# The end of the kernel-spectrum stage of an S4D and mixer block: sums ahead of inverse products, and other PSUM banks for the last pieces

## The chip, the cores and the metric

The kernel runs on one core of one Trainium2 chip. The metric is the device time of one execution in microseconds (us). A core has TensorE (PE; its weight loads are listed as PEld), VectorE (DVE), ScalarE (ACT), GpSimd (POOL) and SyncE (SP, which here only issues DMAs). SBUF is the on-chip memory, and PSUM is the small memory that TensorE writes its results to. A profile is one execution as the hardware profiler recorded it.

## The reference

For a sequence of 2048 tokens with 448 channels, a state-space convolution (S4D) and a token-mixing MLP follow each other, each behind a layer norm with a modulation from a condition vector:

```
dt = exp(log_dt); A = -exp(log_A_real) + 1j * A_imag; C = (C_real + 1j * C_imag) * dt
P = exp((A * dt)[:, :, None] * pos)                    # 448 channels x 256 states x 2048 positions
K = 2 * einsum("dn,dnl->dl", C, P).real                # the convolution kernel of every channel
y = irfft(rfft(h, 4096) * rfft(K, 4096))[:2048] + h * D_skip
x = x + ga * y
h = layernorm(x) * (1 + cb) + sb
x = x + gb * mixer(h)      # layernorm, W1 (2048 x 1792), gelu, W2 (1792 x 2048) along the tokens
```

## The kernel before, in words

**Steps.** The convolution kernel K is made in 56 steps (`NHALF`), two for each of 28 groups of 16 channels. In step s ACT turns two PSUM tiles `xe`, `xg` of phases (pool `pph`, two buffers of two banks each: 4 banks) into sines and cosines (`st_step`, L674), POOL multiplies them into G (L690, L691), DVE into E (L692 to L696), and PE multiplies G and E into `kg` (`st_kgen`, L708; pool `pkg`, 1 bank). After the second step of a group ACT copies `kg` to `ks` (L731), and after each second group POOL adds the skip weights (L737). `st_s1` (L742) then multiplies such a pair of groups into two banks `y` (`y1` in the code) of the pool `pms` (3 banks), whose contents are copied to `yk`, the spectrum of the kernel (L761). `yk` has two chunks of 224 channels; groups 14 to 27, so steps 28 to 55, make the second chunk.

**Pieces.** The product of the spectra and the way back are cut into 32 pieces, 16 for each chunk. Piece n has three parts: the sums `kx` (`pc_s2`, L803, 8 matmuls into one bank of `pms`), the products `z` with the input's spectrum `u` (`pc_mul`, L811, two on DVE), and the inverse products `vv` (`pc_inv`, L821, 8 matmuls) with their copy to `vt` and a DMA to DRAM (`pc_out`, L834). Pieces of the first chunk put `vv` into two banks of `pms` and copy it in two instructions (L842). Pieces of the second put it into a tile of two banks of the pool `pxs` (two buffers) and copy it in one (L839). A piece of the second chunk needs besides a copy of `u` with quarters exchanged (`pc_swap`, L797: two copies on POOL, two on ACT).

**Their order.** PE, ACT, DVE and POOL run in the order of the program. Work that is put off is kept in the lists `dve` and `act`, which `flush` empties at given places of a step; a pair of groups goes to `fresh`, and `mellow` makes it `ready` for `st_s1`. SP's order is chosen by a planner until the second chunk's loop, where from its first round on it is that of the program. The first chunk's pieces run inside steps 33 to 55 by `piece` (L994): an odd step gives the sums of a piece, the next even step its inverse products. The loop over steps (L1081) ran three steps beyond the last (`tail`), in which only pieces and leftovers run. So, in the order of PE:

- step 54: `kg` of step 53, `y` of the pair of groups 24 and 25, `vv` of piece 12 (L1161)
- step 55: `kg` of step 54, `kx` of piece 13
- 56 to 58: `kg` of step 55, then `vv` 13, `kx` 14, `vv` 14, `kx` 15, `y` of the pair 26 and 27, `vv` 15
- second chunk (L1204): `kx` 16, `kx` 17, `vv` 16 and so on

**Loads.** `pc_load(n + 3)` stands ahead of the sums of piece n: `u` (three buffers, 448 KB each, one tile for two pieces in the second chunk) and the table `si` (four buffers, 256 KB). The table of piece n + 4 takes the buffer of piece n, so its load waits for `vv` of n.

After the second chunk come the layer norm and the two products of the mixer, with weights streamed from DRAM (L1270 to L1272, L1433 to L1435).

Of the kernel before, what the change touches and what calls it, by code (L numbers as in the profile page):

```python
# [11 lines left out]
F32 = mybir.dt.float32  # L12
# [4 lines left out]
PSUM = bass.MemoryType.PSUM  # L17
# [5 lines left out]
P = 128  # L23
# [6 lines left out]
NHALF = 2 * NG  # L30
BATCH = 8
DC = 224
NP = 16
# [199 lines left out]
def tile_adaln_s4d_mixer(ctx, tc, i, out):  # L233
# [19 lines left out]
    with ExitStack() as es:  # L253
# [11 lines left out]
        cg, mp, wp = right("cg", 1), right("mp", 8), right("wp", 2)  # L265
        m2p = [right("m2", 3)]
        pms = es.enter_context(tc.tile_pool(name="pms", bufs=3, space=PSUM))
        pph = kgen.enter_context(tc.tile_pool(name="pph", bufs=2, space=PSUM))
        pkg = kgen.enter_context(tc.tile_pool(name="pkg", bufs=1, space=PSUM))
        early = ExitStack()  # L270
        qp = early.enter_context(tc.tile_pool(name="qp", bufs=1))
        mod[0:3] = [qp.tile([P, D], F32, name=f"mod{k}") for k in range(3)]
# [105 lines left out]
        def flush(todo):  # L378
            while todo:
                todo.pop(0)()  # L380
# [323 lines left out]
        def mellow():  # L704
            ready.extend(fresh)
            fresh.clear()
# [32 lines left out]

                act.append(copy)  # L740

        def st_s1(busy):  # L742

            if not ready:
                return False
            p = ready.pop(0)
            c, gl = divmod(p, NG // 4)
            ks = kss.pop(p)
            y1 = [pms.tile([P, 32, 2, 4, 2], F32, tag="ms", name="y1") for _ in range(2)]
            for o in range(2):  # L750
                for m in range(4):
                    for cc in range(2):
                        for q in range(2):
                            r = slice(64 * q, 64 * q + 64)
                            T.matmul(
                                y1[q][64 * cc : 64 * cc + 64, :, o, m], ks[r, o, m], wc[r, cc, r], start=True, stop=True
                            )

            def out(q, copy):
                o = yks[c][:, :, 2 * gl * GD : 2 * (gl + 1) * GD].rearrange("p k (g q m) -> p k g q m", g=2, q=2)  # L760
                copy(o[:, :, :, q], y1[q].rearrange("p k g m b -> p k g (m b)"))  # L761

            for q in range(2):
                (dve if busy else act).append(partial(out, q, V.tensor_copy if busy else S.copy))
            return True


# [22 lines left out]
        def pc_load(n):  # L790
            if n < NP or n % 2 == 0:
                pc_u(n)
            pc_w(n)

        pw = {}

        def pc_swap(n):  # L797

# [20 lines left out]
            pk.pop(n)  # L819

        def pc_inv(n):  # L821
            if n < NP:
                pv[n] = [pms.tile([P, DC], F32, tag="ms", name="vv") for _ in range(2)]
            else:
                pv[n] = pxs.tile([P, 2, 512], F32, tag="vv", name="vv")
            halves_ = pv[n] if n < NP else [pv[n][:, q, 0:DC] for q in range(2)]
            w, z = pl.pop(n), pz.pop(n)
            for t in range(2):
                for b in range(2):
                    for q in range(2):  # L830
                        to, rows = slice(64 * (b ^ q), 64 * (b ^ q) + 64), slice(64 * q, 64 * q + 64)
                        T.matmul(halves_[q][to], w[rows, 1, t, b], z[t][rows, b], start=t == 0, stop=t == 1)  # L832

        def pc_out(n, copy=S.copy):  # L834
            c, p = divmod(n, NP)
            vt = swp.tile([P, 2, DC], F32, tag="vt", name="vt", bufs=4) if c else fp.tile([P, 2, DC], F32, tag="vt", name="vt")
            from_ = pv.pop(n)
            if c:
                copy(vt, from_[:, :, 0:DC])  # L839
# [154 lines left out]
        def piece(go, inside=False):  # L994

            if pieces[1] < pieces[0]:
                n = pieces[1]
                pc_inv(n)
                (dve if inside else act).append(partial(pc_out, n, V.tensor_copy if inside else S.copy))
                pieces[1] += 1  # L1000
            if go:
                n = pieces[0]
                if n + 3 < 2 * NP:
                    pc_load(n + 3)
                pc_s2(n)
                dve.append(partial(pc_mul, n))
                pieces[0] += 1

        def window(s):
# [11 lines left out]
            for e in range(BATCH):  # L1021
# [20 lines left out]
                if s and e < (2 if s <= 32 else 1):  # L1042
                    st_kgen(s - (2 if s <= 32 else 1) + e)
                elif e == 5:
                    if s == 8:
                        yks[0] = y0.tile([P, 32, DC], F32, tag="yk", name="yk0")
                    st_s1(s > 16)
# [29 lines left out]

        WPACE = [[0, 2, 2, 1, 1, 1, 1, 1], [4] * 7 + [8], [4] * 7 + [9], [4] * 8]
        pace = [2] * 32
        tail = NHALF + 3  # L1080
        for s in range(tail):  # L1081
            if s == 32:
                early.close()
                fp = es.enter_context(tc.tile_pool(name="fp", bufs=2))
# [7 lines left out]
                first.close()  # L1092
            if s in late:
                late[s]()
            if s < NHALF and s % BATCH == 0:
                window(s)
                if s == 0:
                    gp_ = right("gp", 3)
# [10 lines left out]
                    more(pace[s])  # L1109

            mellow()
            if s >= NHALF:
                flush(dve)
                mellow()
            else:
                if s < 32 and s % BATCH > 1:
                    st_kgen(s - 2)
                if s % BATCH < 2:
                    warm(10)
                if (s + 1) % BATCH:  # L1120
                    st_phase(s + 1)
                elif s + 1 < NHALF:
                    st_exponents(s + 1)
                if s == 7:
                    warm(10)

                if s > 32 and s % BATCH:
                    st_kgen(s - 1)
                st_step(s, between)
            flush(act)  # L1130
            if s == NHALF:
                st_kgen(s - 1)


            if s in (1, 2):
                x_load(4 + 4 * s, 4, G)
            free = s > 7 and not st_s1(s % BATCH == BATCH - 1)
            if s + 2 < 32 and (s + 2) % BATCH > 1 and s + 2 > 5:
                st_mag2(s + 2)

# [28 lines left out]
        flush(dve)  # L1169
        flush(act)  # L1170
        assert pieces == [NP, NP] and not kss and next(rest, 0) == next(rows, 0) == next(cols, 0) == 0, pieces
# [32 lines left out]
        for k in range(NP + 1):  # L1204
# [262 lines left out]
```

## Time and profile before

| | us |
|---|---|
| three runs | 693.27, 696.14, 698.49 |
| median | 696.14 |
| span of the profiled execution | 693.5 |
| PE busy in it | 628.4 (91%) |
| DVE, ACT, POOL busy | 438.7, 446.6, 269.7 |
| mean granted TensorE clock | 0.968 of full speed |

Of the profiled execution only the span, from its first to its last instruction, is on record, and no time of its own. It lies 0.2 us above the fastest of the three runs and 2.6 us below their median. Busy times are sums over the whole span, in which stages with different limits follow each other; the stage that matters here begins at about 339 us and ends at about 362 us. In a row of a timeline the time in brackets is how long the engine stood idle before the instruction, with the work that released it. A table over stretches of time gives each engine's busy time with the number of its instructions, the granted clock, and the DMA engines' mean busy share.

### The profile page before, as it was taken

How to read it: one execution, taken by the hardware profiler on the slowest of the kernel's cores; microseconds unless marked ns; L12 is line 12 of the kernel's file. 1: busy time of each engine (PE TensorE's matmuls, PEld its weight loads, DVE VectorE, ACT ScalarE, POOL GpSimd, SP SyncE). 2: the span in 40 equal slices, each digit the busy share in tenths (PEclk: the TensorE clock that was granted, in tenths of full speed). 3: DMA queues.
4: the chain of work that ended last, by engine and by line, in shares of the span. 5: the costliest groups of instructions: out<-in, count | busy, mean ns of one | idle time of the engine just before them, and what ended most of it. 6: DMA issues, size and time to landing. Idle time of an engine off the chain costs nothing.

```text
span 693.5 us, 19319 instructions
## 1 busy us (share of the span) xinstructions
PE 628.4 (91%) x7706; PEld 452.3 (65%) x7706; DVE 438.7 (63%) x835; ACT 446.6 (64%) x847; POOL 269.7 (39%) x349
## 2 busy tenths in 40 slices
PE   0878999999888889988898899999999999999997
PEld 0444555444345545555554567778899999999997
DVE  7886789789785574856745578876732364444441
ACT  5888598999689889989856768887322352222220
POOL 7694669588499667767635300000000000000000
PEclk9989999999999899999899999999999999999999
DMA  7595557598786354443479899955574445556540
GB/s 174 176 208 130 196 186 247 200 225 258 219 253 189 94 131 140 131 125 104 116 251 341 280 269 261 262 151 142 177 226 108 146 132 160 160 162 170 163 131 26
DMA packets 100322, 125.16 MB, mean 180 GB/s; under 512 B 13860, under 2 KB 81992, under 8 KB 100232
## 3 DMA queue, kind: packets, MB, share of 16 engines
q1 hardware_dynamic: 99288, 121.30, 61.0%
q0 software_dynamic: 944, 2.62, 1.6%
q8 instruction: 61, 1.00, 0.6%
q14 instruction: 29, 0.24, 0.1%
HBM read 88.53 MB, written 34.87 MB: 178 GB/s over the span
## 4 chain that ended last, share of the span: by engine, by line
PE 62%; ACT 12%; POOL 8%; DMA 6%; DVE 5%; issue 5%; SPq 1%; DVEq 0%; POOLq 0%; ACTq 0%
PE o L1434 7%; PE acc L1270 6%; PE o L1433 6%; PE o L1435 6%; PE acc L1271 6%; PE acc L1272 6%; PE xe L627 5%; PE kg L717 4%; POOL G L691 3%; POOL G L690 2%; PE xg L627 2%; PE vv L832 2%; PE kx L809 2%; PE kg L639 2%; PE y L1307 2%
## 5 line engine op out<-in xcount | busy, mean ns | idle before, releaser
L218 ACT CAST whi<-w 128x896 fp32r<-128x896 f32 x64 | 59.7, 938 | 134.3 <-PE o L1434 82.6
L227 DVE TENSOR_TENSOR wlo<-w,whi 128x896 fp32r<-128x896 f32 x64 | 68.1, 1085 | 40.6 <-ACT whi L218 40.6
L690 POOL TENSOR_TENSOR G<-mag,gs 128x512 f32<-128x512 f32 x56 | 71.8, 1282 | 46.0 <-ACT gs L686 45.9
L1270 PE MATMUL acc<-h3h,whi 128*128 128x448 f32 x224 | 82.9, 370 | 1.7 <-ACT h3h L1337 0.9
L1271 PE MATMUL acc<-h3l,whi 128*128 128x448 f32 x224 | 81.6, 364 | 0.2 <-DVE mean L1291 0.2
L1434 PE MATMUL o<-ul,whi 128*128 128x448 f32 x224 | 81.3, 363 | 0.0
L1433 PE MATMUL o<-uh,whi 128*128 128x448 f32 x224 | 81.2, 362 | 0.0
L1272 PE MATMUL acc<-h3h,wlo 128*128 128x448 f32 x224 | 80.7, 360 | 0.0
L1435 PE MATMUL o<-uh,wlo 128*128 128x448 f32 x224 | 80.6, 360 | 0.0
L717 PEld LDWEIGHTS kg<-E,G 128*32 128x32 f32 x3584 | 58.1, 117 | 31.7 <-issue 22.1
L717 PE MATMUL kg<-E,G 128*32 128x64 f32 x3584 | 68.2, 231 | 4.1 <-issue 4.1
L691 POOL TENSOR_TENSOR G<-mag,gs 128x512 f32<-128x512 f32 x56 | 71.8, 1281 | 0.0
L627 PE MATMUL xg<-tab,lph 64*128 64x512 f32 x112 | 62.9, 561 | 8.0 <-DVE E L696 3.5
L627 PE MATMUL xe<-tab,lph 64*128 64x512 f32 x112 | 63.6, 568 | 1.9 <-ACT gs L687 0.9
L1438 DVE TENSOR_TENSOR y<-o,x 128x448 f32<-128x448 f32 x16 | 10.0, 624 | 78.8 <-PE o L1435 78.8
L692 DVE TENSOR_TENSOR E<-m,xe 128x512 f32<-128x512 f32 x53 | 36.3, 684 | 35.2 <-ACT xe L685 25.1
L671 POOL TENSOR_TENSOR m<-mag,w 128x512 f32<-128x512 f32 x53 | 55.8, 1052 | 4.1
L1270 PEld LDWEIGHTS acc<-h3h,whi 128*128 128x128 f32 x224 | 42.0, 188 | 15.2 <-ACT h L1342 3.5
L817 DVE TENSOR_TENSOR z<-kx,u 128x448 f32<-128x448 f32 x48 | 28.4, 619 | 33.1 <-PE kx L809 30.5
L832 PE MATMUL vv<-z,si 64*64 64x224 f32 x512 | 36.8, 385 | 9.4 <-ACT yk L761 6.2
L627 PE MATMUL xe<-tab,lex 64*128 64x512 f32 x56 | 31.0, 569 | 15.7 <-POOL wm L874 14.8
L1433 PEld LDWEIGHTS o<-uh,whi 128*128 128x128 f32 x224 | 42.1, 188 | 3.4
(242 smaller groups left out, 1455.9 us busy)
## 6 DMA issues: line engine op xcount, KB each, us to landing
w<-in_B_w_dram SPq DMA_DIRECT2D x64, 224.0 KB
w<-in_B_w_dram SPq DMA_DIRECT2D x32, 448.0 KB
yu_d<-yt SPq DMA_DIRECT2D x16, 448.0 KB
yi<-yu_d SPq DMA_DIRECT2D x32, 224.0 KB
us_d<-uo SPq DMA_DIRECT2D x16, 448.0 KB
u<-us_d SPq DMA_DIRECT2D x64, 112.0 KB
v_d<-vt SPq DMA_DIRECT2D x32, 224.0 KB
vt<-v_d SPq DMA_DIRECT2D x14, 448.0 KB
```

Of the source, the lines that this page charges most:

```text
L218: self.nc.scalar.copy(hi, w)
L227: eng.tensor_tensor(lo, w, hi.bitcast(F32), ALU.subtract)
L627: T.matmul(out[k], lhs[r], rhs[r], start=start, stop=stop)
L690: G.tensor_tensor(Gt[:, 1], mg_, v32(sg), ALU.mult)
L691: G.tensor_tensor(Gt[:, 0], mg_, v32(cg_), ALU.mult)
L717: T.matmul(kg[32 * q : 32 * q + 32, m], Gt[:, c, d], E[:, c, d], start=h == 0 and c == 0 and m == 0, stop=h == 1 and c == 1, skip_group_ch ...
L1270: nc.tensor.matmul(acc[f], hi[:, fs], h3h[:, r], start=r == 0, stop=False)
L1271: nc.tensor.matmul(acc[f], hi[:, fs], h3l[:, r], start=False, stop=False)
L1272: nc.tensor.matmul(acc[f], lo[:, fs], h3h[:, r], start=False, stop=r == 15)
L1433: nc.tensor.matmul(o, hi[:, ks], uh[kh][:, k], start=kh == 0 and k == 0, stop=False)
L1434: nc.tensor.matmul(o, hi[:, ks], ul[kh][:, k], start=False, stop=False)
L1435: nc.tensor.matmul(o, lo[:, ks], uh[kh][:, k], start=False, stop=kh == 1 and k == 6)
```

## The change

- The loop ends with step 55 (`range(NHALF)`), and step 54 has no call of `piece`. What steps 55 to 58 did behind `st_step` stands behind the loop as straight code.
- Its order on PE: `kg` of step 54, `kx` 13 (its products now right behind the E products of step 55 on DVE), `kg` of step 55, `vv` 12, `kx` 14, `y` of the pair 26 and 27, `vv` 13, `kx` 15, `vv` 14. `vv` 15 moves into the first round of the second chunk's loop, behind `kx` 16.
- `pkg` moves to the other side of PSUM, and the phases' four banks are given up after step 55 (`phases.close()`). `pxs` takes them at once, and pieces 12 to 15 put their `vv` there and copy it in one instruction.
- The last two copies of `yk` are divided, one on DVE, one on ACT; they were both on ACT.

```diff
-        pph = kgen.enter_context(tc.tile_pool(name="pph", bufs=2, space=PSUM))
-        pkg = kgen.enter_context(tc.tile_pool(name="pkg", bufs=1, space=PSUM))
+        pkg = kgen.enter_context(tc.tile_pool(name="pkg", bufs=1, space=PSUM, side="right"))
+        phases = ExitStack()
+        pph = phases.enter_context(tc.tile_pool(name="pph", bufs=2, space=PSUM))
...
-        def st_s1(busy):
+        def st_s1(*to):
...
             for q in range(2):
-                (dve if busy else act).append(partial(out, q, V.tensor_copy if busy else S.copy))
+                to[-q].append(partial(out, q, S.copy if to[-q] is act else V.tensor_copy))
...
         def pc_inv(n):
-            if n < NP:
-                pv[n] = [pms.tile([P, DC], F32, tag="ms", name="vv") for _ in range(2)]
+            if wide:
+                pv[n] = wide[0].tile([P, 2, 512], F32, tag="vv", name="vv")
+                halves_ = [pv[n][:, q, 0:DC] for q in range(2)]
             else:
-                pv[n] = pxs.tile([P, 2, 512], F32, tag="vv", name="vv")
-            halves_ = pv[n] if n < NP else [pv[n][:, q, 0:DC] for q in range(2)]
+                pv[n] = halves_ = [pms.tile([P, DC], F32, tag="ms", name="vv") for _ in range(2)]
...
-            if c:
+            if not isinstance(from_, list):
                 copy(vt, from_[:, :, 0:DC])
...
-        tail = NHALF + 3
-        for s in range(tail):
+        for s in range(NHALF):
...
                 st_step(s, between)
+            if s == NHALF - 1:
+                break
             flush(act)
-            if s == NHALF:
-                st_kgen(s - 1)
...
-            if s > 32:
-                piece(pieces[0] < NP and (s % 2 == 1 or s >= NHALF))
+            if s > 32 and s != NHALF - 2:
+                piece(s % 2 == 1)
...
+        def forth(n):
+
+            if n + 3 < 2 * NP:
+                pc_load(n + 3)
+            pc_s2(n)
+            pc_mul(n)
+
+        def back(n):
+
+            pc_inv(n)
+            pc_out(n)
+
+        def settle():
+
+            flush(dve)
+            flush(act)
+            flush(dve)
+            mellow()
+            mellow()
+
+        phases.close()
+        pxs = es.enter_context(tc.tile_pool(name="pxs", bufs=2, space=PSUM))
+        wide.append(pxs)
+        n = pieces[0]
+        assert pieces == [NP - 3, NP - 4]
+        forth(n)
         flush(act)
+        st_kgen(NHALF - 1)
+        settle()
+        back(n - 1)
+        forth(n + 1)
+        st_s1(dve, act)
+        for f in dve + act:
+            f()
+        dve.clear()
+        act.clear()
+        back(n)
+        forth(n + 2)
+        back(n + 1)
         kgen.close()
-        pxs = es.enter_context(tc.tile_pool(name="pxs", bufs=2, space=PSUM))
...
-            if k:
-                pc_inv(n - 1)
-                pc_out(n - 1)
+            back(n - 1)
```

More of the change, by code (lines that the diff above doesn't have):

```diff
@@ L793, in pc_load @@
             pc_w(n)
-        pw = {}
+        pw, wide = {}, []
         def pc_swap(n):
@@ L1046, in window @@
                         yks[0] = y0.tile([P, 32, DC], F32, tag="yk", name="yk0")
-                    st_s1(s > 16)
+                    st_s1(dve if s > 16 else act)
                 for k, e0 in ((4, 1), (5, 3), (3, 6)) if s == 16 else ():
@@ L1094, in tile_adaln_s4d_mixer @@
                 late[s]()
-            if s < NHALF and s % BATCH == 0:
+            if s % BATCH == 0:
                 window(s)
@@ L1111, in tile_adaln_s4d_mixer @@
             mellow()
[L1112 to L1115, printed above, removed]
+            if True:
                 if s < 32 and s % BATCH > 1:
@@ L1129, in tile_adaln_s4d_mixer @@
                 st_step(s, between)
+            if s == NHALF - 1:
+                break
             flush(act)
-            if s == NHALF:
-                st_kgen(s - 1)
             if s in (1, 2):
                 x_load(4 + 4 * s, 4, G)
-            free = s > 7 and not st_s1(s % BATCH == BATCH - 1)
+            free = s > 7 and not st_s1(dve if s % BATCH == BATCH - 1 else act)
             if s + 2 < 32 and (s + 2) % BATCH > 1 and s + 2 > 5:
@@ L1168, in tile_adaln_s4d_mixer @@
                 nc.sync.dma_start(b2, i["B_b2"].rearrange("(t p) -> p t", p=P))
-        flush(dve)
-        flush(act)
-        assert pieces == [NP, NP] and not kss and next(rest, 0) == next(rows, 0) == next(cols, 0) == 0, pieces
+        def forth(n):
[18 more added lines that the diff above has]
+        forth(n)
+        flush(act)
+        st_kgen(NHALF - 1)
[10 more added lines that the diff above has]
+        back(n + 1)
+        assert not kss and next(rest, 0) == next(rows, 0) == next(cols, 0) == 0
         kgen.close()
-        pxs = es.enter_context(tc.tile_pool(name="pxs", bufs=2, space=PSUM))
         wst = WeightStream(tc, ctx, i)
```

## Prediction

> **What bounds the kernel now.** I read the page first, then a table of stages, then the timeline from step 54 to the second chunk engine by engine, and last the granted clock in stretches of 3.41 us and the DMA share. In the tables a row gives the stretch, its length, then PE, PEld, DVE, ACT and POOL busy us with their instructions, the granted TensorE clock, the DMA share and GB/s.
>
> ```profile
> span 693.5 us, 19319 instructions
> ...
> 344.60:357.60 13.00, 11.92 (x274) 7.45 (x269) 3.47 (x6) 3.23 (x9) 2.41 (x5) 0.81 0.61 193
> ...
> 405.00:550.00 145.00, 144.20 (x698) 122.51 (x699) 90.10 (x216) 82.72 (x158) 0.00 (x0) 1.00 0.72 193
> ```
>
> From 405 us on PE is the bound (144.2 of 145 us), so a start that comes earlier comes out at the end. The change acts between the last products of step 55 (about 344.6) and the first sums of the second chunk, kx of piece 16 (357.58). In these 13 us PE looks busy, but at a clock of 0.81, while DVE, ACT and POOL are nearly empty. The timeline shows why (start, us, engine, line, work, idle before and its releaser):
>
> ```profile
> 338.49 1.10 PE L717 MATMUL kg<-E,G 128*32 128x64 f32 x64
> ...
> 340.89 0.68 DVE L696 TENSOR_TENSOR E<-m,xg 128x512 f32<-128x512 f32 x1
> 342.92 1.10 ACT L761 COPY yk<-y 128x512 f32<-128x512 f32 x2
> 343.59 1.76 PE L832 MATMUL vv<-z,si 64*64 64x224 f32 x14 [2.50 <-ACT yk L761]
> 343.66 0.68 DVE L696 TENSOR_TENSOR E<-m,xg 128x512 f32<-128x512 f32 x1
> 343.32 1.28 POOL L691 TENSOR_TENSOR G<-mag,gs 128x512 f32<-128x512 f32 x1
> 345.28 1.93 PE L717 MATMUL kg<-E,G 128*32 128x64 f32 x64
> 347.15 1.76 PE L809 MATMUL kx<-yk,si 128*64 128x224 f32 x8
> 348.84 1.46 PE L717 MATMUL kg<-E,G 128*32 128x64 f32 x64
> 350.22 0.99 PE L832 MATMUL vv<-z,si 64*64 64x224 f32 x16
> 350.37 0.37 ACT L731 COPY ks<-kg 128x256 f32<-128x256 f32 x1 [4.38 <-PE kg L717]
> 350.82 0.21 POOL L737 TENSOR_TENSOR ks<-ks,dsk 128x8 f32<-128x8 f32 x1 [6.22 <-ACT ks L731]
> 351.14 0.98 PE L809 MATMUL kx<-yk,si 128*64 128x224 f32 x8
> 352.17 1.16 DVE L817 TENSOR_TENSOR z<-kx,u 128x448 f32<-128x448 f32 x2 [2.05 <-PE kx L809]
> 354.82 1.16 PE L755 MATMUL y<-wc,ks 64*64 64x64 f32 x64
> 356.03 1.07 ACT L761 COPY yk<-y 128x512 f32<-128x512 f32 x2 [1.36 <-PE y L755]
> 356.24 1.41 PE L832 MATMUL vv<-z,si 64*64 64x224 f32 x16 [0.26 <-DVE z L817]
> 357.58 1.73 PE L809 MATMUL kx<-yk,si 128*64 128x224 f32 x16
> 358.36 3.45 ACT L801 COPY sw<-u 32x448 f32<-32x448 f32 x6
> 359.58 0.62 DVE L817 TENSOR_TENSOR z<-kx,sw 128x448 f32<-128x448 f32 x1 [0.34 <-ACT sw L801]
> 360.26 1.15 POOL L801 COPY sw<-u 32x448 f32<-32x448 f32 x2 [3.71 <-DVE z L817]
> 361.82 0.53 ACT L839 COPY vt<-vv 128x448 f32<-128x448 f32 x1
> ```
>
> The reader is to see one wait and its long tail. Inverse products of piece 12 (343.59) wait 2.50 us: the pool pms has three banks, the sums of piece 12 and the two banks of y had them, and the second bank for vv comes free only when ACT, which first has the whole sine chain of step 55 to do, copies yk. Behind that matmul stand, in PE's order, the kg products of step 54, whose E was ready at 341.57 (340.89 + 0.68). Everything then runs at half speed (64 kg matmuls 1.93 us against 1.10) until about 349.6, and the kg products of step 55, ready at 344.60 (POOL's 343.32 + 1.28), end at 350.3 instead of 345.7. After them come the copy of ks, POOL's addition, y, yk. The clock in detail:
>
> ```profile
> 339.42:342.83 3.41, 1.67 (x79) 1.17 (x67) 3.37 (x6) 3.21 (x8) 2.37 (x3) 1.00 0.39 105
> 342.83:346.24 3.41, 2.65 (x50) 1.74 (x54) 1.35 (x3) 1.78 (x5) 1.77 (x2) 0.50 0.14 39
> ...
> 192.64:196.06 3.42, 1.93 (x30) 0.75 (x28) 3.42 (x6) 3.31 (x8) 3.34 (x4) 1.00 1.05 299
> 196.06:199.47 3.41, 3.41 (x120) 2.00 (x114) 3.07 (x6) 1.78 (x4) 3.33 (x5) 1.00 1.09 318
> ```
>
> PE busy 1.67 us of a stretch is followed by half clock, 1.93 us is not. Between these lies the threshold that I use below.
>
> **The change part by part.** I lay out the new order on PE from the times above, with 1.10 us for a kg group and y (1.16, of which the next group hides some), and 0.93 us from one kx or vv group to the next (350.22 to 351.14 gives 0.92).
>
> *Step 54 without a piece.* The inverse products of piece 12 leave the place where they stalled. The kg products of step 54 start at 341.6 and end at 342.7; the sums of piece 13, put ahead of the inverse products, follow to 343.6 (the bank of kx 12 is free once its products are done, which stand on DVE ahead of the E row of 340.89). PE then waits for G of step 55 (344.60). PE is busy about 2.0 us in any 3.41 us here, above 1.93, so I take full clock. Price if not: one stretch of 3.41 us at half speed, 1.7 us.
>
> *After step 55.* kg of step 55 344.65 to 345.7; vv 12 to 346.65; kx 14 to 347.6; y to 348.65; vv 13 to 349.6; kx 15 to 350.5; vv 14 to 351.45; kx 16 from 351.45. Side work: the products of piece 13 on DVE right behind E (344.34 to 345.5, before 348.96); ks on ACT 345.8 to 346.2, POOL's addition to 346.4, 1.2 us before y wants it; products of piece 14 347.65 to 348.8, piece 15 350.55 to 351.7. The copies of yk are split, one on DVE (behind the products of 14), one on ACT, and end at 349.5; kx 16 reads them 2 us later. So none of these is on the path while PE goes from group to group. The same work took until 357.58: 6.1 us earlier.
>
> *The phases' banks as buffers.* vv 12 to 15 get two pairs of banks of their own. They are free when E of step 55 is done (344.34), before vv 12 (345.7). That removes the wait of vv 15 for yk (356.24, 1.41 us) too. One copy of 128x448 (0.53 us, the 361.82 row) takes the place of two; four pieces save a fraction of a us of ACT that is idle anyway. I price the addresses and the moved kg bank at nothing; nothing on the path waits for a bank of that side.
>
> *Piece 15 goes into the second chunk's loop.* Its inverse products follow kx 16 on PE and its copy follows the swaps of 17 on ACT. PE: kx 16 to 352.4, vv 15 to 353.3, kx 17 to 354.2. ACT: vt 14 to 352.05, two swaps of 16 (3.45 us for six, 0.575 each) to 353.2, so the swapped product of 16 starts at 353.25 against 359.58 (6.3 earlier); swaps 17 to 354.35, vt 15 to 354.9, swaps 18 to 356.05, vt 16 at 356.05 against 361.82 (5.8 earlier). POOL's swap of 18, which waits for the product of 16, comes at 353.95 against 360.26 (6.3). I take the smallest, **5.8 us**. Of it 2.7 us is clock: from 343.59 to 350.22 are 6.63 us for work that at full speed takes about 3.9.
>
> *The transfers.* SP issues the loads of the second chunk when a buffer comes free, so they come earlier as well but closer together.
>
> ```profile
> 345.60:351.40 5.80, 5.80 (x155) 4.17 (x146) 1.16 (x2) 0.90 (x4) 0.21 (x1) 0.65 0.37 96
> 351.40:361.00 9.60, 8.17 (x146) 4.58 (x144) 4.36 (x8) 5.29 (x13) 2.90 (x6) 1.00 0.96 337
> ...
> 369.50:391.50 22.00, 20.06 (x250) 10.73 (x246) 11.98 (x20) 16.98 (x31) 11.02 (x20) 0.92 1.03 365
> ```
>
> ```profile
> 350.14 0.33 SPq L777 DMA_DIRECT2D u<-us_d  x1
> ...
> 354.21 2.34 POOL L801 COPY sw<-u 32x448 f32<-32x448 f32 x4 [3.18 <-DMA si<-in_SJ_dram]
> ```
>
> ```profile
> 365.22 0.36 SPq L777 DMA_DIRECT2D u<-us_d  x1
> ...
> 371.29 1.13 ACT L801 COPY sw<-u 32x448 f32<-32x448 f32 x2 [3.57 <-DMA u<-us_d]
> ```
>
> ```profile
> si<-in_SJ_dram SPq DMA_DIRECT2D x10, 256.0 KB
> u<-us_d SPq DMA_DIRECT2D x5, 448.0 KB
> v_d<-vt SPq DMA_DIRECT2D x8, 224.0 KB
> ```
>
> Three u (16, 18, 20), five tables and four pieces of v are 3.5 MiB, about 3.6 MB: 9.9 us at the 365 GB/s of the row. The first, u 16, can go out when the products of 13 end: 345.5 instead of 350.14, only 4.6 us earlier. So they end near 355.4, and kx 19, the last that needs one of them, is due at 356.9 by the order above. It just fits, with 0.37 of the DMA's time in use where the work is moved to, but table 17 (free at 349.6, wanted at 353.3) has 3.7 us and tables 18 and 19 about 3.6, where u 16 took at most 4.1 to be used. I bound the toll by 0 and by landings of 6.1 us (365.22 to 371.29): 2.4 us. I take **0.7**, near the first, since 4.1 is the row of this same place. The Trainium skill, "DMA: Bandwidth & Descriptors", section Specifications, gives about 358 GB/s from HBM for one core. By that the bytes would take 10.1 us, an estimate, and the sum would change by 0.2 us. The trace has 365 over 22 us, and I keep it.
>
> The gap of the old order also meets a rule on the clock. The Trainium skill, "TensorE: Matmul & The Clock Gate", section "What you observe" and the table of states behind it, has the clock halved after an idle window of about 3.4 us. By that the 2.50 us wait would have cost no clock, and the sum would lose its 2.7 us. The 0.50 behind a stretch that was busy 1.67 of 3.41 us says otherwise, and the row decides.
>
> **The sum.** 5.8 - 0.7 = 5.1 us. Against the profiled execution that is 693.5 - 5.1 = 688.4; the median of the runs, 696.14, lies 2.6 above that span, so the forecast is 696.1 - 5.1 = **691.0**. A measurement of this kernel can tell about 1% (7 us) from no change, so my likeliest result is "within 1%", though a real gain.
>
> **The rivals.**
>
> *The DMA takes the place of the wait* (gain 1 to 3.5, time about 693.8). Landings of 6.1 us hold kx 17 to 19 by 2.4 us, and the idle PE may add 1.7 us of half clock: 5.8 - 4.1 = 1.7 at worst. For it: from 369.50 on the share is 1.03, and ACT and POOL wait 3.57 us for u. Against: before 351.4 the share is 0.37. Chance 0.18.
>
> *More than the sum* (gain over 7, time about 688). The shift moves u 22, and its wait of 3.57 us with the half clock behind it shrinks: 6.3 + 1.7 = 8.0. For it: SP issued u 22 late, at 365.22, behind other loads. Against: the same loads stand ahead of it. Chance 0.13.
>
> *Slower: the second chunk's tables.* SP issues in order; the table of 16 waits for vv 12, which now comes behind step 55, and tables 17 to 19 wait for vv 13 to 15, each now only one or two groups ahead of its reader. If one of these stands ahead of u 16 or u 18 in SP's order, PE, ACT and DVE wait together. It decides from landings of 8.5 us: kx 17 would start at 349.6 + 8.5 = 358.1 instead of 353.3, 4.8 lost, and 1.7 of clock with it, 6.5 in all: 0.7 us slower, 696.8. For: 6.1 us was seen. Against: that was with the DMA at 1.0. Chance 0.06.
>
> *The change does not do what it says:* the stall of vv 12 only moves into the wait for G of step 55, and the rest is given back later by a bound that the stage does not show; time 696. Chance 0.03.
>
> **How the numbers follow.** Forecast 0.60, the rivals 0.18, 0.13, 0.06 and 0.03. Gains from 1.7 to 8.0 give 694.4 to 688.1; the median of three runs between 693.27 and 698.49 can itself be off by about 1 us, so the range is 687.0 to 695.0, which leaves out the slower cases and a little at the lower end. Faster by over 1% (below 689.2): the third case, 0.13, and the top of the forecast's own spread, 0.09: 0.22. Slower by over 1% (above 703.1) needs twice the slower rival's price: 0.02. Within 1%: 0.76.
>
> **What would show it.** Right: no wait of vv behind yk at step 54; kg of step 54 directly behind y; clock 1.00 from 340 to 357; kg of step 55 done by 346; kx 16 near 351.5, about 7 us behind the last G of step 55 (before 13.0); the swapped product of 16 near 353.3; the start of the PE-bound part about 5 us earlier. Wrong: half clock in that stretch; kx 17 to 19 released by a table; a shift at kx 16 that has shrunk by more than 2 us at 405.

## The result, and the profile after

The changed kernel takes 690.2 us (median of 20 runs, 687.81 to 695.01), the kernel before 696.12 us (20 runs, 690.38 to 700.53). The ratio is 0.9931, with a 95% interval of 0.9911 to 0.9952, so 3.3 to 6.2 us are gained. The forecast was 691.0 us.

The profiled execution of the changed kernel has a span of 691.5 us and took 693.27 us, 3.1 us above the median. In all 20 runs the span is 1.7 to 1.9 us shorter than the time. So the profiled execution of the kernel before, with its span of 693.5 us, took about 695.3 us (an estimate) and lies some 0.8 us below its median, not 2.6; the forecast, which goes by the median, stays. The ratios below leave out runs that took more than 1.5% longer than the fastest of their kernel, and the profiles of no54 and stall54 are of two such runs, so I read them only up to kx 16.

Two profiled executions of the changed kernel (the second is after2, below) reach the end of step 55 at times 4.5 us apart, so I read all positions from one mark that every trace has: the end of POOL's last G of step 55. It is at 344.60 us before (343.32 + 1.28), and after at 342.22 and 337.72 us. A number behind kx, vv or vt is that of the piece: kx 16 are the sums of piece 16, the first of the second chunk. FL are the loads into the tile `fl` (L1267); in SP's order they stand behind the write of v of piece 16, and so they go out 2.2 to 2.3 us behind the copy vt 16 in before, after, after2, halftab_vt4 and best. Here are rows of the timeline after, from step 54 to the second chunk, for all engines:

```profile
339.32 1.49 PE L718 MATMUL kg<-E,G 128*32 128x64 f32 x64 [1.03 <-DVE E L697]
340.74 0.98 PE L810 MATMUL kx<-yk,si 128*64 128x224 f32 x8
340.94 1.28 POOL L692 TENSOR_TENSOR G<-mag,gs 128x512 f32<-128x512 f32 x1
341.86 1.15 DVE L818 TENSOR_TENSOR z<-kx,u 128x448 f32<-128x448 f32 x2
342.27 1.10 PE L718 MATMUL kg<-E,G 128*32 128x64 f32 x64 [0.56 <-POOL G L692]
343.30 0.99 PE L833 MATMUL vv<-z,si 64*64 64x224 f32 x16
345.13 1.16 PE L756 MATMUL y<-wc,ks 64*64 64x64 f32 x64
346.34 0.69 DVE L762 COPY yk<-y 128x512 f32<-128x512 f32 x1
347.83 0.38 SPq L847 DMA_DIRECT2D v_d<-vt  x1
349.19 0.98 PE L810 MATMUL kx<-yk,si 128*64 128x224 f32 x8 [0.32 <-DVE z L818]
349.81 0.53 ACT L840 COPY vt<-vv 128x448 f32<-128x448 f32 x1 [2.16 <-DMA v_d<-vt]
350.36 2.29 ACT L802 COPY sw<-u 32x448 f32<-32x448 f32 x4
351.59 0.62 DVE L818 TENSOR_TENSOR z<-kx,sw 128x448 f32<-128x448 f32 x1 [0.76 <-ACT sw L802]
352.66 0.98 PE L810 MATMUL kx<-yk,si 128*64 128x224 f32 x8 [1.57 <-DMA si<-in_SJ_dram]
353.40 0.53 ACT L840 COPY vt<-vv 128x448 f32<-128x448 f32 x1 [0.75 <-DMA v_d<-vt]
355.12 0.53 ACT L840 COPY vt<-vv 128x448 f32<-128x448 f32 x1
355.25 0.98 PE L810 MATMUL kx<-yk,si 128*64 128x224 f32 x8 [0.69 <-DMA si<-in_SJ_dram]
357.37 1.04 SPq L1267 DMA_DIRECT2D fl<-in_FL_dram  x2
```

The same loads before:

```profile
364.08 1.04 SPq L1236 DMA_DIRECT2D fl<-in_FL_dram  x2
```

Two things are to be seen. First, the stall is gone: kg of step 54 waits only for its own E, the sums of piece 13 follow, kg of step 55 starts 0.05 us behind the mark, and kx 16 stands at 349.19, which is 6.97 us behind the mark where it was 12.98. Second, waits that the stage did not have have come in behind it: the copies vt 14 (349.81) and vt 15 (353.40) wait until an earlier v has been written to DRAM, and kx 17 and 18 wait for their tables.

The 13 us behind the mark in the table of stretches, the whole way from the mark to the last inverse product of piece 31 before and after, and the first matmul of the mixer (first start in the last two rows, which are of before and after):

```profile
342.22:355.22 13.00, 10.39 (x240) 6.47 (x240) 6.14 (x11) 6.55 (x13) 5.28 (x9) 1.00 0.86 278
```

```profile
344.60:391.76 47.16, 43.67 (x659) 24.36 (x655) 22.56 (x38) 29.92 (x58) 20.53 (x35) 0.91 0.88 294
```

```profile
342.22:387.10 44.88, 38.23 (x595) 21.23 (x596) 22.95 (x40) 29.51 (x54) 20.53 (x35) 1.00 0.95 309
```

```profile
L1270 PE MATMUL acc<-h3h,whi x224: 360/362/476, 404.4 to 554.5; 128*128 128x448 f32 x112
```

```profile
L1301 PE MATMUL acc<-h3h,whi x224: 360/363/476, 400.2 to 552.5; 128*128 128x448 f32 x112
```

The clock in the stage is 1.00 where it was 0.81, and the DMA share in it 0.86 where it was 0.61. From the mark to the last inverse product only 2.28 us are left of the 6.0 (47.16 - 44.88), and the mixer starts 1.8 us sooner behind the mark (59.8 against 58.0). A second profile of the changed kernel, below, keeps 3.8 and 4.8 us.

From the mark to the end of the span there are 348.9 us before, 349.3 in this profile and 344.9 in the second. In the first 15.6 us of the mixer PE is busy 15.42 us before, 13.62 in this profile and 14.72 in the second, so part of an earlier start is lost again there. In this profile nothing of the shift is left at the end, and its span is 2.0 us shorter than that of the kernel before only because the mark itself comes 2.4 us earlier, for which the change gives no reason. That the kernel became faster is shown by the times of the 20 runs, not by this one pair of profiles.

### The profile page after: what moved, and what is told of

It reads as the page before. It is cut to its first block, busy times and chain, and to the rows that moved or that the text cites. A ratio compares the mean times of both kernels' runs of the same rounds, so it can differ in the third digit from the quotient of the medians.

```text
span 691.5 us, 19311 instructions
## 1 busy us (share of the span) xinstructions
PE 619.8 (90%) x7706; PEld 448.4 (65%) x7706; DVE 438.9 (63%) x836; ACT 445.7 (64%) x842; POOL 269.4 (39%) x349
## 4 chain that ended last, share of the span: by engine, by line
PE 57%; ACT 13%; DMA 11%; DVE 7%; POOL 6%; issue 5%; SPq 1%; POOLq 0%; DVEq 0%; ACTq 0%
PE o L1464 7%; PE o L1466 6%; PE o L1465 6%; PE acc L1301 6%; PE acc L1302 6%; PE acc L1303 6%; PE kg L718 4%; PE xe L628 4%; DMA u<-us_d 2%; ACT mag L651 2%; PE pu L586 2%; DMA w<-in_B_w_dram 2%; PE xg L628 2%; DMA vt<-v_d 2%; POOL G L691 1%
## 5 line engine op out<-in xcount | busy, mean ns | idle before, releaser
L718 PE MATMUL kg<-E,G 128*32 128x64 f32 x3584 | 66.6, 229 | 6.7 <-issue 4.4
L628 PE MATMUL xe<-tab,lph 64*128 64x512 f32 x112 | 62.2, 555 | 1.8 <-ACT gs L688 0.9
L628 PE MATMUL xe<-tab,lex 64*128 64x512 f32 x56 | 30.8, 564 | 16.0 <-DMA lex<-wm 15.6
L684 ACT ACTIVATE ab<-xe 128x512 f32<-128x512 f32 x56 | 34.0, 607 | 16.8 <-PE xg L628 11.8
L1302 PEld LDWEIGHTS acc<-h3l,whi 128*128 128x128 f32 x224 | 42.0, 187 | 3.5 <-DVE h3l L1375 0.7
```

What stands on the lines that cost most here:

```text
L628: T.matmul(out[k], lhs[r], rhs[r], start=start, stop=stop)
L718: T.matmul(kg[32 * q : 32 * q + 32, m], Gt[:, c, d], E[:, c, d], start=h == 0 and c == 0 and m == 0, stop=h == 1 and c == 1, skip_group_ch ...
L1302: nc.tensor.matmul(acc[f], hi[:, fs], h3l[:, r], start=False, stop=False)
```

## The experiments

All positions are us behind the last G of step 55, from one profile each: start of kx 16, issue of the loads of FL, end of the last inverse product, start of the mixer's matmuls. Where the expectations give a position to the POOL memset (19.48 before, 15.15 after), it is that of FL; the memset itself starts at 16.76 and 11.15. The ratio is that of times to the kernel before, run beside it, from 12 runs of each new kernel (6 for vt4 and halftab_vt4).

| kernel | ratio (95%) | kx 16 | FL | last vv | mixer |
|---|---|---|---|---|---|
| before | 1 | 12.98 | 19.48 | 47.16 | 59.8 |
| changed | 0.9931 (0.9911 to 0.9952) | 6.97 | 15.15 | 44.88 | 58.0 |
| after2, the same again | 0.9944 (0.9912 to 0.9976) | 7.40 | 15.05 | 43.35 | 55.0 |
| no54 | 0.9947 (0.9912 to 0.9982) | 10.39 | | | |
| filler | 0.9964 (0.9928 to 1.0001) | 10.23 | 16.72 | 44.78 | 57.7 |
| stall54 | 0.9972 (0.9937 to 1.0007) | 8.88 | | | |
| pmsbanks | 0.9973 (0.9941 to 1.0006) | 7.99 | 14.87 | 43.43 | 54.9 |
| halftab_b | 0.9984 (0.9955 to 1.0014) | 11.79 | 18.28 | 48.08 | 58.2 |
| halftab_a | 0.9936 (0.9902 to 0.9969) | 7.26 | 14.73 | 42.19 | 53.9 |
| early_u | 0.9943 (0.9911 to 0.9975) | 7.24 | 14.95 | 42.84 | 56.4 |
| vt4 | 0.9898 (0.9852 to 0.9945) | 7.47 | 14.67 | 43.08 | 54.9 |
| tab6 | 0.9939 (0.9905 to 0.9973) | 6.58 | 15.01 | 44.03 | 55.1 |
| halftab_vt4 | 0.9864 (0.9805 to 0.9923) | 7.20 | 13.57 | 40.02 | 51.8 |
| best | 0.9928 (0.9895 to 0.9962) | 6.59 | 13.51 | 42.41 | 55.3 |

**The stall alone.** no54 takes the piece out of step 54 and changes nothing else:

```diff
-            if s > 32:
+            if s > 32 and s != NHALF - 2:
                 piece(pieces[0] < NP and (s % 2 == 1 or s >= NHALF))
```

> The kernel before with one edit: no piece in step 54, so the inverse products of piece 12 come in step 55, behind the kg products of step 54; all else, PSUM banks too, as before. Theory (the stall in front of the kg products and the half clock behind it are over half of the gain): last kg products about 3.8 us earlier against the last G of step 55 (end about 2 us behind it, before 5.7), full clock in that stretch, time 0.4 to 0.6% under before. Rival (the later order and the banks make the gain, the stall only shifts): last kg products earlier by under 1 us, time within 0.2% of before.

```profile
344.95 1.38 PE L832 MATMUL vv<-z,si 64*64 64x224 f32 x16
346.26 0.98 PE L809 MATMUL kx<-yk,si 128*64 128x224 f32 x8
347.17 1.10 PE L717 MATMUL kg<-E,G 128*32 128x64 f32 x64
356.76 1.73 PE L809 MATMUL kx<-yk,si 128*64 128x224 f32 x16 [1.13 <-DMA si<-in_SJ_dram]
```

The mark is at 346.37. The last kg products end at 1.9 us (347.17 + 1.10 - 346.37), 3.8 us earlier than before, and every group runs at full clock. kx 16 is only 2.6 us earlier: of the 3.8, 1.13 us are already lost to the table of piece 16. In time it is 3.7 us (0.0053 of 694.93, the median of the kernel before beside it), most of the 4.8 that the whole change gives, though the interval, 1.3 to 6.1 us, is wide. The theory holds, and the rival falls.

**The clock alone.** filler leaves the stall and its order and fills it with matmuls that nobody reads:

```diff
+            if s == NHALF - 2:
+                warm(20)
             if s > 32:
                 piece(pieces[0] < NP and (s % 2 == 1 or s >= NHALF))
```

> The kernel before with 20 idle matmuls (results used by nobody) between y and the inverse products of piece 12 in step 54, about 2 us of work in the wait; the order is otherwise that of before, and the wait for the copies of yk stays. Theory (the half clock is 2.7 us of the loss): clock 1.00 from step 54 to the second chunk, last kg products 2 to 3 us earlier against the last G, time 0.2 to 0.4% under before. Rival (the order alone counts, PE has slack here): the clock is full and the last kg products end no earlier, time as before.

```profile
340.34 2.36 PE L639 MATMUL kg<-ones 128*128 128x256 bf16 x20
342.63 1.67 PE L832 MATMUL vv<-z,si 64*64 64x224 f32 x16
344.22 1.10 PE L717 MATMUL kg<-E,G 128*32 128x64 f32 x64
346.16 1.10 PE L717 MATMUL kg<-E,G 128*32 128x64 f32 x64
```

The mark is at 344.33. kg of step 54 takes 1.10 us in place of 1.93, and kx 16 comes at 10.23 in place of 12.98: 2.75 us for the clock alone, where 2.7 had been worked out. Work that does nothing brings kx 16 forward; in time it is 2.5 us, with an interval that just touches no change, so that the kernel as a whole becomes faster by it is not shown.

**The rest with the stall put back.** stall54 is the changed kernel with the inverse products of piece 12 in step 54 and in banks of pms:

```diff
-            if s > 32 and s != NHALF - 2:
+            if s > 32:
                 piece(s % 2 == 1)
...
-        assert pieces == [NP - 3, NP - 4]
+        assert pieces == [NP - 3, NP - 3]
...
         settle()
-        back(n - 1)
```

> The changed kernel with the piece of step 54 put back: inverse products of piece 12 in step 54 with banks of pms, where they wait for yk; the rest of the change stays. Theory: the 2.5 us wait and, behind it, half clock are back; the first sums of the second chunk come 10 to 11 us behind the last G of step 55 (after 7.0, before 13.0), time 0.2 to 0.4% under before. Rival (the tail is what counts): 7 to 8 us, and time 0.6 to 0.7% under before, as with the whole change.

```profile
343.51 1.76 PE L833 MATMUL vv<-z,si 64*64 64x224 f32 x14 [2.51 <-ACT yk L762]
345.20 1.70 PE L718 MATMUL kg<-E,G 128*32 128x64 f32 x64
346.83 0.98 PE L810 MATMUL kx<-yk,si 128*64 128x224 f32 x8
```

The wait is back to 0.01 us, but half clock ends within the next kg group, not two groups later, and kx 16 comes at 8.88, earlier than the 10 to 11 that I expected and later than the 7 to 8 of the rival. The length of the half clock behind one and the same gap differs from run to run. halftab_b, below, has the order of the kernel before up to kx 16, and it shows this too:

```profile
338.09 0.98 PE L835 MATMUL vv<-z,si 64*64 64x224 f32 x14 [2.51 <-ACT yk L761]
339.00 1.61 PE L717 MATMUL kg<-E,G 128*32 128x64 f32 x64
340.54 1.76 PE L812 MATMUL kx<-yk,si 128*64 128x224 f32 x8
```

The wait is the same 2.51 us, but half clock lasts for one stretch of 3.41 us (339.41 to 342.82), where the profile before has two (342.83 to 349.65), and kx 16 comes at 11.79 and not at 12.98. So the 2.7 us that were worked out and the 2.75 of filler rest on one and the same profile of the kernel before, one with long half clock; against halftab_b filler gains 1.6 us. In time stall54 is 1.9 us under before, as expected; its interval reaches no change.

**The banks.** pmsbanks keeps the order and puts vv 12 to 14 into banks of pms again:

```diff
         phases.close()
         pxs = es.enter_context(tc.tile_pool(name="pxs", bufs=2, space=PSUM))
-        wide.append(pxs)
...
         kgen.close()
+        wide.append(pxs)
```

> The changed kernel, its order kept, but the inverse products of pieces 12 to 14 in two banks of pms again, with two copies each. Theory (the banks are worth something of their own): y waits for the copies of vt 12, vv 13 for those of yk, vv 14 for those of vt 13, each 0.6 to 0.9 us; the first sums of the second chunk come 9 to 9.5 us behind the last G (after 7.0), time 0.3 to 0.45% under before. Rival (order is all): under 8 us and time 0.6 to 0.7% under before.

```profile
344.49 1.46 PE L833 MATMUL vv<-z,si 64*64 64x224 f32 x16 [0.26 <-DVE z L818]
348.16 0.98 PE L810 MATMUL kx<-yk,si 128*64 128x224 f32 x8 [0.39 <-PE vv L833]
```

The banks are worth 0.6 to 1.0 us at kx 16 (7.99 against 7.40 and 6.97 in the two profiles of the changed kernel), where I had expected 2 to 2.5: y had no wait, since vt 12 was copied while PE was at kx 14. The loads of FL go out as early as in the changed kernel, 14.87, so nothing of it is left one stage later. The time is 0.27% under before, less than either theory had, and its interval, from 0.6% under to no change, decides nothing.

**The same again.** after2 is the changed kernel, for a second profile.

> The changed kernel once more, for a second profile of it beside the others of this call. Theory (the second chunk is bound by transfers and gives part of the shift back): the first sums of the second chunk again 7.0 us behind the last G of step 55 (before 13.0), tables 17 to 19 again late by 0.5 to 2 us each or together, so that its POOL memset and the loads behind it come 4 to 5 us earlier than before, not 6; start of the mixer's matmuls 55 to 58 us behind the last G (before 59.8); time 0.6 to 0.8% under before. Rival (the 1.8 us that the first profile kept at the mixer is the true gain): mixer at 58, time 0.3% under.

```profile
337.72:350.72 13.00, 10.39 (x240) 6.47 (x240) 6.13 (x11) 6.64 (x13) 4.83 (x8) 1.00 0.84 275
...
391.76:404.39 12.63, 10.04 (x42) 6.21 (x42) 5.96 (x17) 6.45 (x14) 0.00 (x0) 0.86 0.77 219
...
387.10:400.22 13.12, 10.09 (x42) 5.97 (x42) 5.92 (x17) 6.13 (x13) 0.00 (x0) 0.87 0.71 207
...
381.07:392.71 11.64, 8.55 (x42) 5.12 (x42) 5.92 (x17) 6.13 (x13) 0.00 (x0) 1.00 0.74 199
```

The first and the last row are of this profile, the second of the kernel before, the third of the first profile of the changed kernel; the last three rows go from the last inverse product to the mixer. kx 16 is at 7.40, since it waits 0.75 us for its own table. FL is at 15.05 again, so 4.4 us are kept there in both. The mixer starts 4.8 us earlier than before, not 1.8. Half of the distance between the two profiles is a stretch of half clock ahead of the mixer that one has and the other has not (13.12 us at 0.87 against 11.64 us at 1.00). The kernel before has such a stretch too (12.63 us at 0.86), so about 1 us of the 4.8 is that after2 was spared one. Of the shift itself 2.3 and 3.8 us are kept at the last inverse product. Against the rival, that 1.8 us is the true gain, speak the times of the changed kernel, of which the interval begins at 3.3 us; the profiles alone don't decide it.

**Fewer transfers.** Both kernels, without the tables of the second chunk's odd pieces, which use the table of the piece ahead:

```diff
         def pc_w(n, pool=None):
             c, p = divmod(n, NP)
+            if c and p % 2:
+                pl[n] = pl[n - 1]
+                return
```

> The kernel before, leaving out the tables of the second chunk's odd pieces: those use the table of the piece ahead of them, so 8 of 16 loads of 256 KB are gone and every other table is there long ago. Theory (transfers bound the second chunk): the chunk, from the POOL memset to the last inverse product, takes 24 to 26 us in place of 27.7, and the time falls by 1 to 3 us. Rival (compute bounds it): 27 us or more, time as before.

> The changed kernel with the same tables left out, those of the second chunk's odd pieces. Theory (the DMA is what gives part of the shift back): no wait for a table at kx 17 to 19, the POOL memset 13.5 to 14 us behind the last G (after 15.15, before 19.48), and the distance to the kernel before with the same left out is 5.5 to 6 us, more than the 4.8 of the whole kernels. Rival (something else gives it back: the copies' buffers, the order on ACT): memset at 15 us or later, distance 4.8 us or less.

The kernel before, from FL to the last inverse product, with these tables left out:

```profile
357.37:387.17 29.80, 26.99 (x319) 13.66 (x312) 15.42 (x27) 21.31 (x38) 14.39 (x27) 0.89 0.91 281
```

It gains 0.0016, which is no change that can be measured, and this stretch takes 29.8 us against 27.7 (47.16 - 19.48) with all tables. That is a miss for the theory that transfers alone bound the old chunk; the clock of 0.89 lengthens it here (0.94 with all tables), so it doesn't refute that the DMA has a part. In the changed kernel the tables of 17 to 19 are no longer waited for, yet FL comes at 14.73, not at 13.5 to 14. The distance between the two kernels in time is 3.3 us (0.0048), not 5.5 to 6, but their intervals overlap, and this one says little. So there was another cause, the one that the rival named. The timeline after shows it: pc_out of the first chunk takes its tile from a pool with two buffers. vt 15 needs the one of vt 13, whose v was issued at 347.83, and could start only at 353.40, 5.6 us later. ACT waits, and behind vt 15 in its order stand the swaps of 18, and behind these vt 16. In halftab_a itself it is vt 14 that waits for the write of v 12:

```profile
351.00 0.53 ACT L843 COPY vt<-vv 128x448 f32<-128x448 f32 x1 [2.45 <-DMA v_d<-vt]
```

**The buffers of vt, and of the tables.**

```diff
-            vt = swp.tile(...) if c else fp.tile([P, 2, DC], F32, tag="vt", name="vt")
+            vt = swp.tile(...) if c else fp.tile([P, 2, DC], F32, tag="vt", name="vt", bufs=4)
```

> The changed kernel with four buffers in place of two for vt of the first chunk, so that vt 14 and vt 15 don't wait until v of pieces 12 and 13 has been written. Theory now (these two waits, 2.8 us on ACT in both profiles, are a part of what was given back, the late tables of 17 to 19 the other): vt 15 comes 1 to 1.5 us earlier (9.5 to 10 us behind the last G, after 11.2), the swaps of 18, the POOL memset and the loads behind it 0.5 to 1 us earlier (14.0 to 14.6, after 15.1), time 0 to 0.15% under the changed kernel. Rival (tables alone): vt 15 earlier, memset where it was.

```diff
-            w = (pool or fp).tile([P, 2, 2, 2, 64], F32, tag="si", name="si", bufs=2 if pool else 4)
+            w = (pool or fp).tile([P, 2, 2, 2, 64], F32, tag="si", name="si", bufs=2 if pool else 6)
```

> The changed kernel with six buffers in place of four for the tables, so that those of 16 to 19 don't wait for the inverse products of 12 to 15 and go out before the last G. Theory now: no wait for a table at kx 16 to 19; kx 18 at 12 us behind the last G (after 13.0); the later tables are late as before, since the DMA is full from there on; memset at 14.3 to 14.8, time 0 to 0.2% under the changed kernel. Rival (the DMA engines are full already between 7 and 17 us, so earlier issues only reorder): u 16 or u 18 late in the tables' place, memset at 15 or later.

> The changed kernel, leaving out the tables of the second chunk's odd pieces as above, and with four buffers for vt of the first chunk. Theory now (tables and these buffers together are what was given back): memset 13.4 to 13.8 us behind the last G (19.48 before; with the 5.8 us worked out, 13.7), vt 16 at 11.2 to 11.6. Rival (a third cause): memset still at 14.5 or later.

ACT's vt 15 of vt4 (mark 340.80), then vt 14 and 15 of tab6 (mark 344.92), then vt 15 and 16 of halftab_vt4 (mark 343.43):

```profile
350.39 0.53 ACT L840 COPY vt<-vv 128x448 f32<-128x448 f32 x1
```

```profile
352.47 0.53 ACT L840 COPY vt<-vv 128x448 f32<-128x448 f32 x1 [2.12 <-DMA v_d<-vt]
...
355.96 0.53 ACT L840 COPY vt<-vv 128x448 f32<-128x448 f32 x1 [0.64 <-DMA v_d<-vt]
```

```profile
353.03 0.53 ACT L843 COPY vt<-vv 128x448 f32<-128x448 f32 x1
354.75 0.53 ACT L843 COPY vt<-vv 128x448 f32<-128x448 f32 x1
```

With four buffers vt 15 comes at 9.6 in place of 11.2, but kx 16 waits 0.81 and kx 17 1.09 us for their tables, and FL moves by 0.5 only. With six table buffers kx 16 to 18 wait for no table (6.58, 8.40, 10.55), but vt 14 and 15 wait, and FL stays at 15.01. Each hides the other. With both gone (halftab_vt4) vt 16 is at 11.3 and FL at 13.57: 5.9 us earlier than before, where the prediction's working without a toll had 5.8. This close agreement is in part luck, since against halftab_b (18.28) it is 4.7. Among the profiles of the changed kernel, which have full clock in this stage, the reading is firm: FL is at 14.95 to 15.15 with both waits there (after, after2, early_u), at 14.67 to 15.01 with one of them gone (vt4, halftab_a, tab6), and at 13.5 to 13.6 with both gone (halftab_vt4, and best below, which does the whole work). That settles what took the 1.5 us between kx 16 and FL: the two waits together. vt4 has the lowest ratio of the kernels that do the whole work; its interval overlaps that of the changed kernel, and its profile ends the chunk 0.3 us ahead of after2, so that it beats the change is not shown.

**Earlier loads, and a version with all three.** early_u takes this edit; best takes it with `bufs=3` for vt and `bufs=5` for the tables:

```diff
-                if k % 2 == 0 and n + 4 < 2 * NP:
+                if k == 0:
                     pc_u(n + 4)
...
                 pc_mul(n)
+                if k % 2 and n + 5 < 2 * NP:
+                    pc_u(n + 5)
```

> The changed kernel with one edit in the second chunk: u of a pair of pieces is loaded half a round earlier, right behind the last product that reads its buffer, ahead of the copy of v, of the loads of x and of FL in SP's order. Theory (u waits in SP's queue, not for its buffer): u 22 goes out 3 us earlier, the wait for it (3.1 us on ACT) shrinks by 2 to 3 us, and the time falls by 1 to 3 us under the changed kernel, 0.8 to 1.1% under before. Rival (the DMA engines are full, so an earlier issue only pushes others back): another load is late by as much, time as the changed kernel.

> The changed kernel with u loaded half a round earlier (the edit of the kernel with early u), three buffers for vt of the first chunk and five for the tables. Theory now (start of the second chunk 1 us earlier, one wait for u gone; the rest of the chunk is full of transfers): memset at 14 to 14.5 us behind the last G, last inverse product 41.5 to 42.5 (after 44.9 and 43.4), time 0.7 to 1.0% under before, 0.1 to 0.4% under the changed kernel. Rival (all of it only reorders transfers): last inverse product at 43 or later, time as the changed kernel.

From FL to the last inverse product, in after2, best and halftab_vt4:

```profile
352.77:381.07 28.30, 26.35 (x347) 14.03 (x340) 16.59 (x29) 21.40 (x39) 13.75 (x25) 1.00 1.01 340
```

```profile
351.81:380.71 28.90, 25.20 (x330) 13.50 (x332) 15.68 (x26) 20.86 (x39) 14.45 (x27) 1.00 1.05 345
```

```profile
357.00:383.45 26.45, 24.57 (x325) 13.27 (x324) 15.91 (x27) 20.87 (x38) 14.13 (x26) 1.00 0.98 310
```

best starts as early as halftab_vt4 (FL at 13.51, earlier than the 14 to 14.5 expected), the tables of 16 to 18 are in time, and yet it ends its chunk at 42.41 and not at 40.02: kx 19 waits for its table,

```profile
352.39 0.98 PE L810 MATMUL kx<-yk,si 128*64 128x224 f32 x8 [1.80 <-DMA si<-in_SJ_dram]
```

and with the DMA engines at 1.05 and 345 GB/s its 28.9 us are 2.4 us longer than those of the kernel that has 2 MiB less to move. Its time is that of the changed kernel (0.9928 against 0.9931). So transfers are one bound of the new kernel from FL on. That they are the only one is not shown: halftab_a, which has the same 2 MiB less to move, is only 0.8 us shorter there than after2 (27.5 against 28.3). A start 1.5 us earlier gave 0.9 us at the chunk's end, which is less than the 1.5 us by which the two profiles of the changed kernel differ there, and nothing that can be told in the time. early_u sends u 22 out 3.5 us earlier (12.7 behind the mark, after2 16.2), and ACT then waits 2.83 us for a later u: the chunk ends at 42.84, the ratio is 0.9943. So its rival holds.

## Why the prediction came out right, step by step

- *Step 54 and the clock*: right. Full clock came as worked out from the busy share, kx 16 is 6.0 us earlier against the mark in one profile and 5.6 in the other (6.1 forecast), filler gives 2.75 us for the clock (2.7 forecast), and no54 ends kg 3.8 us earlier. All of these are taken against the one profile that the prediction was made from. Against halftab_b, with half as much half clock behind the same wait, kx 16 is 4.4 to 4.8 us earlier, so the sizes came out so well partly by luck.
- *The side work*: right for DVE, for ks and for the divided copies of yk (begun at 346.34, 2.9 us ahead of kx 16).
- *The phases' banks*: the direction was right; they are worth 0.6 to 1.0 us at kx 16 by pmsbanks. The moved bank of kg, which the prediction prices at nothing, has no run of its own. The mark lies at 339.1 to 346.4 us in the four profiles with kg in its old place and at 337.7 to 344.9 in the ten with kg moved, so that it changed the time of the earlier steps is neither shown nor refuted.
- *"Piece 15 goes into the second chunk's loop ... ACT: vt 14 to 352.05, two swaps of 16 ... to 353.2"*: this step failed. It has ACT copy vt 14 as soon as vv 14 is done, and overlooks that the tile has two buffers and waits for a write to DRAM: vv 14 ended at 348.87, vt 14 began at 349.81. In the old order vv 13 and vv 15, which share a buffer, lay 6.0 us apart (350.22 and 356.24), and vt 15 waited for no write; in the new one they are 4 us apart (346.05 and 350.10), less than the 4.9 and 5.6 us from the issue of a write to the next use of its buffer. The swapped product of 16 came 5.6 us earlier and not 6.3 (359.58 - 344.60 against 351.59 - 342.22), vt 16 4.3 and not 5.8 (17.2 against 12.9).
- *The transfers, 0.7 us*: too small, and one cause of two. The bounds of 0 to 2.4 us held at FL, where 1.5 of the 5.9 us are missing (4.3 and 4.4 kept). Behind FL more is lost: at the last inverse product 2.3 and 3.8 us of the shift are left in the two profiles, a toll of 3.5 and 2.0 against the 5.8, the first above the bound of 2.4. The DMA has a part in it, as best shows; that it is all of it is argued. Two of the signs that the prediction gave for being wrong did come: kx 17 and 18 waited for a table (1.57 and 0.69 us), and in the first profile the shift shrank by more than 2 us, from 6.0 at kx 16 to 1.8 at the mixer (in the second from 5.6 to 4.8).
- *"a start that comes earlier comes out at the end"*: only partly. The mixer's first 15.6 us were not PE-bound in the first profile (13.62 us busy), and at the end of the span 0 and 4.0 us were left in the two profiles.
- *The sum*: 5.1 us forecast, 4.8 by the ratio. The term of 5.8 was right for a kernel without these waits (5.9 in halftab_vt4, against the same profile before); the toll was about twice the 0.7 at the start of the chunk and three to five times it at its end. That 5.1 and 4.8 lie so close is therefore luck in part: the interval is 3.3 to 6.2 us, and no profile shows how the 4.8 come about behind the chunk.
- *The rivals*: the DMA as the new bound is what partly happened (its gain of 1 to 3.5 us fits the first profile at the last inverse product, and of the time only the lower end of the interval); no table was so late that the kernel became slower.

What stays open is how much of the shift an average run keeps past the second chunk. The two profiles keep 1.8 and 4.8 us at the mixer, and half of that distance is half clock ahead of the mixer, which comes and goes between runs; of the whole kernel before there is one profile only.

## What to carry to other kernels

A wait of PE costs its length and, where it left a stretch of 3.41 us more than half empty (PE busy 1.67 us before, 1.30 and 1.31 in stall54 and halftab_b), also half clock for some of the work behind it (3.4 to 6.8 us here); look at what stands behind it in PE's order first. When a stage is made shorter, go through every pool that it uses and ask what releases a buffer: one that a write to DRAM releases was free only 4.9 and 5.6 us behind the issue here, and the stage had become shorter than that. And work out the bytes of the stage that follows, since a start that comes earlier can be lost again to the transfers behind it (in best, kx 19 waits 1.80 us for its table).

## What the runs showed of the hardware

The half clock came behind a gap of 2.50 us, and 20 idle matmuls (2.36 us) in that gap kept it away. The rule that the prediction took from the Trainium skill ("TensorE: Matmul & The Clock Gate", "What you observe" and the table behind it), an idle window of about 3.4 us, read as a stretch without any matmul, would have had the filler change nothing; kx 16 came 2.75 us earlier.

The same gap (2.50 and 2.51 us) cost two kg groups and the kx between them at half speed in one profile, and only the next kg group in another (1.70 us, the kx behind it 0.98). In the first PE was busy 2.65 us of the first half-speed stretch of 3.41 us, and a second one followed; in stall54 (343.11 to 346.52) it was busy 3.01 us and in halftab_b 3.41, and full clock followed. Of the three, half clock went on behind the stretch that was busy least.

A write of 224 KB that was issued at 347.83 let its buffer be used again only 5.6 us later, and one issued at 344.96 4.9 us later, with the DMA engines at a share of 0.86 over the stage.
